# Batch 0's first keys through SyncE's queue in fp32, cast by VectorE, and another order of batch 0's last chunks

## The chip, the core and the metric

The kernel runs on one core of one Trainium2 chip. A core has a matmul engine (TensorE, "PE" in the profile; its weight loads are listed as "PEld"), VectorE ("DVE"), ScalarE ("ACT"), GpSimd ("POOL") and SyncE ("SP"). Sixteen DMA engines serve the core. GpSimd and SyncE each issue transfers into a queue of their own. The metric is the time on the device in microseconds (us): of the kernel before there are six runs, and their median is 365.86 us (365.17 to 366.24).

## The reference

Two blocks follow each other. The first is causal attention over 8 batches and 8 heads, with 576 queries and 64 values per head; 16 extra "beacon" keys and values, that every query may see, stand ahead of the 576 keys. The second is a feed-forward block on the 4608 tokens.

```python
k_all = np.concatenate([beacon_k, k], axis=2)
v_all = np.concatenate([beacon_v, v], axis=2)
scores = q @ k_all^T / sqrt(64)            # causal on the 576 keys
a = softmax(scores)
x = (a @ v_all), heads side by side        # 4608 x 512
out = (gelu(x @ w_gate) * (x @ w_val)) @ w_out     # 512 -> 1536 -> 512
```

All inputs and the output are fp32. The kernel computes in bf16 and accumulates in fp32.

## The kernel before, in words

The heads of a batch are taken two at a time: pair `m` is heads 2m and 2m+1, one on partitions 0 to 63 and one on 64 to 127. For a pair the kernel needs queries and keys with the head's 64 dimensions on partitions, so they are transposed. Batch 0 has nothing before it that could hide this, and so it is done by matmuls against an identity: `load_qk6` (its transfers go through `dma`, L111, on GpSimd's queue, and turn fp32 into bf16 on the way) brings two heads of q or k into `qk6` as 96 partitions of 6 rows; `tr_part` makes twelve transposes of it (L176) and one more for the beacon keys; `transpose_half` copies the outcome from PSUM into `qkT`, by VectorE (L213), or for pair 0's queries by ScalarE (through the helper at L171); `beacon_part` (L217) copies the 16 beacon columns. `transpose_both(b, m)` does keys first, then queries. Where ScalarE makes the copy, `transpose_half` puts eight transposes of a zero tile (`idle`) in front, whose outcome nobody reads.

A score tile is written by `scores`, called `c` for batch 0. A pair's causal triangle is cut into four chunks: `(m, 0)` to `(m, 2)` are 512, 496 and 464 columns for each of two heads, `(m, 3)` is 208 columns, and `(0, 3), (1, 3)` share one tile. TensorE computes the chunk and adds the mask by small matmuls with `eye` and `neg`; ScalarE then takes the exponential of the whole tile (L171). `av_head` multiplies the exponentials of one head with the values, `av` those of both heads of a pair; VectorE divides by the sum (L332, L334). `turn` transposes the normalised pair back, `put` copies it into `xT_sb`, from which the feed-forward matmuls (`gv_mms`) read.

PSUM sets what may run ahead: score tiles, the tiles of `av` and the tiles of `gv_mms` take turns in the pool `psum_s` with three buffers; a new one waits until the reader of the third before it is done. `psum_t` and `psum_o` have one buffer each, for transposes and for `av_head`.

The order on every engine is the order in which the program is written (`keep`). At the start it is this. SyncE issues the beacon keys and values of batch 0 in fp32 (L474, L476). GpSimd issues k of heads 0 and 1, q of heads 0 and 1, k of heads 2 and 3, then makes `eye` (the identity, L480), then goes on with q of heads 2 and 3, the other four loads of q and k, five loads of v, and the weights. VectorE clears tiles, casts the two beacon tiles (L517, L518) and makes `neg` from `eye` (L519, L520). TensorE runs 66 matmuls on the zero tile (`warm(66)`) and then pair 0's transposes. From there on chunks and transposes of the four pairs alternate, as written out by hand in the diff's last part. The rest of the program, 8 batches in which attention and feed-forward matmuls alternate, is not touched.

Of the kernel before, what the change touches and what calls it, by code (L numbers as in the profile page):

```python
# [7 lines left out]
P = 128  # L8
B, H, S, NB, D = 8, 8, 576, 16, 64
SK = S + NB  # L10
N_TOK = B * S
D_MODEL = 512
# [28 lines left out]
FP32 = mybir.dt.float32  # L41
# [8 lines left out]
def kernel(  # L50
# [12 lines left out]
    nc = tc.nc  # L63
    keep = tc.keep_in_program_order
# [8 lines left out]
    opool = ctx.enter_context(tc.tile_pool(name="opool", bufs=2))  # L73
    psum_s = ctx.enter_context(tc.tile_pool(name="psum_s", bufs=3, space=bass.MemoryType.PSUM))
    psum_t = ctx.enter_context(tc.tile_pool(name="psum_t", bufs=1, space=bass.MemoryType.PSUM))
# [16 lines left out]
    q_ring, k_ring, v_ring = [], [], []  # L92
# [17 lines left out]
    def dma(out_ap, in_ap):  # L110
        keep(nc.gpsimd.dma_start(out=out_ap, in_=in_ap))  # L111

    qk6 = {}

    def qk6_of(b):
        if b not in qk6:
            qk6[b] = (
                hpool.tile([P, 2, H, 6 * D], BF16, name="qk6", tag="hT_sb"),
                kpool.tile([NB, H, D], BF16, name="kb", tag="kb"),
            )  # L120
        return qk6[b]

    def load_qk6(b, h0, h1, ws=(1, 0)):
        for w in ws:
            src = (q, k)[w]
            dma(
                qk6_of(b)[0][0:96, w, h0:h1, :],
                src[b, h0:h1, :, :].rearrange("h (p r) d -> p h (r d)", r=6),
            )
# [37 lines left out]
    def mm(out_ap, lhsT, rhs, start, stop, **kw):  # L167
        keep(nc.tensor.matmul(out_ap, lhsT, rhs, start=start, stop=stop, **kw))  # L168

    def act(out_ap, in_ap, func, **kw):  # L170
        keep(nc.scalar.activation(out_ap, in_ap, func, **kw))  # L171


    def tr(out_ap, in_ap):
        n = in_ap.shape[0]
        keep(nc.tensor.transpose(out_ap, in_ap, ident[0:n, 0:n]))  # L176

    def tr_part(b, m, w, dst):
        qk, kb = qk6[b]
        for r in range(6):  # L180
            for hi in range(2):
                tr(
                    dst[64 * hi : 64 * hi + 64, r * 96 : (r + 1) * 96],
                    qk[0:96, w, 2 * m + hi, r * D : (r + 1) * D],
                )
        if w:
            tr(dst[:, S:SK], kb[:, 2 * m : 2 * m + 2, :])
# [14 lines left out]
    def transpose_half(b, m, w, by_act=False):  # L202
        pool, tag = ((psum_o, "o"), (psum_t, "t"))[w]
        t_ps = pool.tile([P, 1024], BF16, name="t_ps", tag=tag)
        for _ in range(8 if by_act else 0):
            tr(t_ps[0:D, 640:768], idle[:, 0:D])
        tr_part(b, m, w, t_ps)
        out_ap = qkT[:, m, w, NB:SK].rearrange("p (t r) -> p t r", r=6)
        in_ap = t_ps[:, 0:S].rearrange("p (r t) -> p t r", r=6)
        if by_act:  # L210
            act(out_ap, in_ap, ACT.Copy)
        else:
            keep(nc.vector.tensor_copy(out_ap, in_ap))  # L213
        return t_ps

    def beacon_part(m, t_ps):
        keep(nc.vector.tensor_copy(qkT[:, m, 1, 0:NB], t_ps[:, S:SK]))  # L217

    def transpose_both(b, m):
        k_ps = transpose_half(b, m, 1)  # L220
        transpose_half(b, m, 0, by_act=m == 0)
        beacon_part(m, k_ps)

    def warm(n):
        w_ps = psum_s.tile([P, 2, 512], FP32, name="w_ps", tag="s")
        for j in range(n):
            mm(w_ps[:, 0, 0:D], idle[:, 0:P], idle[:, 0:D], True, True)
# [10 lines left out]
    def scores(b, *parts):  # L238
        s_ps = psum_s.tile([P, 2, 512], FP32, name="s_ps", tag="s")
        c0 = 0  # L240
        for m, c in parts:
            score_mms(b, m, c, s_ps[:, :, c0 : c0 + CHUNK_W[c]])
            c0 += CHUNK_W[c]
        (m, c), n = parts[0], len(parts)
        o, w = CHUNK_OFF[c], CHUNK_W[c]
        act(
            exp_ring[:, m : m + n, :, o : o + w].rearrange("p g h c -> p h g c"),
            s_ps[:, :, 0 : n * w].rearrange("p h (g c) -> p h g c", g=n),
            ACT.Exp,
            scale=QK_SCALE,  # L250
        )
        if b:
            for m, c in parts:
                masks(b, m, c)
# [54 lines left out]
    def attend(b, m, hi, x_ps):  # L309
        expT, v_sb = exp_ring[:, m, :, :], v_ring[b % NRING]  # L310
        for j in range(5):
            for t in range(j + 1):
                e0 = EXP_OFF[t] + (j - t) * P
                mm(
                    x_ps[:, j * DV : (j + 1) * DV],
                    expT[0 : KROWS[t], hi, e0 : e0 + P],
                    v_sb[0 : KROWS[t], t, 2 * m + hi, 0:DV],
                    t == 0,
                    t == j,
                    skip_group_check=True,  # L320
                )
# [3 lines left out]
    def normalize(b, m, x_ps, h0, h1):  # L325
        i = b * NPAIR + m
        if h0 == 0:
            y_of[i] = ypool.tile([P, 5, 2, D], BF16, name="y_sb", tag="y_sb")
        r_sb = npool.tile([P, 2, 5, 1], FP32, name="r_sb", tag="r_sb")
        x = x_ps[:, :, 0 : 5 * DV].rearrange("p b (j d) -> p b j d", d=DV)  # L330
        r = r_sb[:, h0:h1, :, :]
        keep(nc.vector.reciprocal(r, x[:, :, :, D:DV]))  # L332
        keep(
            nc.vector.tensor_tensor(  # L334
                out=y_of[i][:, :, h0:h1, :].rearrange("p j b d -> p b j d"),
                in0=x[:, :, :, 0:D],
                in1=r.to_broadcast([P, h1 - h0, 5, D]),
                op=ALU.mult,
            )
        )  # L340

    def av(b, m):
        x = psum_s.tile([P, 2, 512], FP32, name="x_ps", tag="s")
        for hi in range(2):
            attend(b, m, hi, x[:, hi, :])
        normalize(b, m, x, 0, 2)

    def av_head(b, m, hi, pool, tag):
        x = pool.tile([P, 1, 512], FP32, name="x_ps", tag=tag)
        attend(b, m, hi, x[:, 0, :])  # L350
        normalize(b, m, x, hi, hi + 1)
# [108 lines left out]
    def out_mms(ci, u0, u1):  # L460
        for u in range(u0, u1):
# [8 lines left out]
                if ci >= N_CHUNKS - 2:  # L470
                    store(nc.sync)

    kb_sb = opool.tile([NB, H, D], FP32, name="kb_sb", tag="o_sb")
    keep(nc.sync.dma_start(out=kb_sb, in_=beacon_k[0].rearrange("h t d -> t h d")))  # L474
    vb_sb = opool.tile([NB, H, D], FP32, name="vb_sb", tag="o_sb")
    keep(nc.sync.dma_start(out=vb_sb, in_=beacon_v[0].rearrange("h t d -> t h d")))  # L476
    load_qk6(0, 0, 2)
    load_qk6(0, 2, 4, (1,))
    keep(
        nc.gpsimd.affine_select(  # L480
            out=eye,
            in_=eye,
# [4 lines left out]
            channel_multiplier=-1,  # L487
        )
    )
    load_qk6(0, 2, 4, (0,))  # L490
    load_qk6(0, 4, 6)
    load_qk6(0, 6, H)
    for load in key_loads(v, beacon_v, v_ring[0][:, :, :, 0:D], 0)[1:]:
# [18 lines left out]
    def c(*parts):  # L512
        scores(0, *parts)

    keep(nc.scalar.preload_act_table_set(SET_EXP))
    warm(66)
    keep(nc.vector.tensor_copy(qk6[0][1], kb_sb))  # L517
    keep(nc.vector.tensor_copy(v_ring[0][0:NB, 0, :, 0:D], vb_sb))  # L518
    keep(nc.vector.tensor_tensor_scan(neg, eye, idle, -1.0, ALU.add, ALU.add))  # L519
    keep(nc.vector.tensor_scalar_mul(neg, neg, -MASKED))  # L520
    transpose_both(0, 0)
    c((0, 0))
    c((0, 2))
    transpose_both(0, 1)
# [8 lines left out]
    c((2, 2))  # L533
    c((2, 1))
    c((3, 0))
    c((3, 2))
    av_head(0, 0, 0, psum_t, "t")
    av_head(0, 0, 1, psum_o, "o")
    c((2, 3), (3, 3))
    av(0, 1)  # L540
    c((3, 1))
    av(0, 2)
    turn(0, 0)
    put(0, 0, by_act=True)
# [123 lines left out]
```

The softmax here doesn't subtract the row's maximum and nothing guards it: scores larger than these inputs give would overflow.

## Time and profile before

| What | Value |
|---|---|
| median of six runs | 365.86 us |
| the profiled execution's own time | 365.73 us |
| its span, first to last instruction | 363.9 us |
| TensorE busy | 357.2 us, 98% of the span |
| ScalarE, GpSimd, VectorE busy | 52%, 44%, 43% |
| TensorE on the chain that ended last | 97% |
| TensorE busy from 0 to 21.84 us (before the first feed-forward matmul) | 18.4 of 21.84 us |
| TensorE busy from 21.84 us on | 338.9 of 342.2 us |

The span leaves out what lies before the first and after the last instruction, 1.8 us in this execution. A row of the timeline gives the start in us, the time taken (of all instructions merged into the row), the engine, the line, the operation and its tiles out<-in, and, in brackets, how long the engine sat idle before it and what ended that. Transfers are listed where they are issued; the time to landing runs from the start of the issue.

### The profile page before, as it was taken

How to read it: one execution, taken by the hardware profiler on the slowest of the kernel's cores; microseconds unless marked ns; L12 is line 12 of the kernel's file. 1: busy time of each engine (PE TensorE's matmuls, PEld its weight loads, DVE VectorE, ACT ScalarE, POOL GpSimd, SP SyncE). 2: the span in 40 equal slices, each digit the busy share in tenths (PEclk: the TensorE clock that was granted, in tenths of full speed). 3: DMA queues.
4: the chain of work that ended last, by engine and by line, in shares of the span. 5: the costliest groups of instructions: out<-in, count | busy, mean ns of one | idle time of the engine just before them, and what ended most of it. 6: DMA issues, size and time to landing. Idle time of an engine off the chain costs nothing.

```text
span 363.9 us, 7670 instructions
## 1 busy us (share of the span) xinstructions
PE 357.2 (98%) x3170; PEld 184.7 (51%) x3170; DVE 155.3 (43%) x305; ACT 189.0 (52%) x243; POOL 161.3 (44%) x288
## 2 busy tenths in 40 slices
PE   7899999999999999999999999999999999999996
PEld 7664446444654455444644464446544554444443
DVE  4546546343453335443534354334444353333332
ACT  3963488237923594349623891379335953321210
POOL 8934487555536552846374554556330530000000
PEclk9999999999999999999999999999999999999999
DMA  8999999899169954999299927993795032000103
GB/s 108 177 204 204 195 120 97 123 171 193 26 126 141 215 51 73 151 210 83 57 142 207 130 38 118 167 195 35 112 144 126 19 65 111 0 0 31 58 35 111
DMA packets 160419, 41.57 MB, mean 114 GB/s; under 512 B 146944, under 2 KB 155904, under 8 KB 160384
## 3 DMA queue, kind: packets, MB, share of 16 engines
q0 software_dynamic: 104848, 19.11, 68.6%
q1 hardware_dynamic: 55536, 21.96, 29.6%
q8 instruction: 25, 0.41, 0.5%
q14 instruction: 10, 0.08, 0.1%
HBM read 38.27 MB, written 9.44 MB: 131 GB/s over the span
## 4 chain that ended last, share of the span: by engine, by line
PE 97%; DVE 2%; issue 0%; ACT 0%; DVEq 0%
PE gv_ps L168 48%; PE o_ps L168 26%; PE x_ps L168 9%; PE s_ps L168 8%; PE t_ps L176 2%; PE v_ps L168 2%; PE g_ps L168 2%; DVE qkT L213 1%; PE w_ps L168 1%; PE y_ps L176 0%; DVE hT_sb L426 0%; ACT qkT L171 0%; DVE o_sb L445 0%; DVE qkT L217 0%; DVE idle L80 0%
## 5 line engine op out<-in xcount | busy, mean ns | idle before, releaser
L171 ACT ACTIVATE ge_sb<-gv_ps 128x512 bf16<-128x512 f32 x101 | 59.4, 597 | 142.8 <-PE gv_ps L168 141.7
L426 DVE TENSOR_TENSOR hT_sb<-gv_ps,ge_sb 128x512 bf16<-128x512 f32 x101 | 69.0, 691 | 113.5 <-ACT ge_sb L171 111.1
L168 PE MATMUL gv_ps<-xT_sb,wg_sb 128*128 128x512 bf16 x404 | 111.5, 379 | 0.0
L168 PE MATMUL gv_ps<-xT_sb,wv_sb 128*128 128x512 bf16 x404 | 111.5, 379 | 0.0
L168 PE MATMUL o_ps<-wo_sb,hT_sb 128*128 128x512 bf16 (+2 forms) x444 | 104.7, 373 | 0.0
L171 ACT ACTIVATE expT<-s_ps 128x992 bf16<-128x992 f32 (+3 forms) x112 | 100.6, 974 | 5.9 <-PE s_ps L168 4.7
L298 POOL TENSOR_SCALAR_AFFINE_SELECT expT<-expT 128x256 bf16<-128x256 bf16 (+1 forms) x140 | 52.3, 392 | 48.2 <-ACT expT L171 46.0
L168 PEld LDWEIGHTS <-wv_sb 128*128 128x128 bf16 x432 | 42.2, 98 | 50.6
L168 PEld LDWEIGHTS <-wg_sb 128*128 128x128 bf16 x432 | 42.0, 98 | 50.0
L168 PEld LDWEIGHTS <-hT_sb 128*128 128x128 bf16 x444 | 39.9, 98 | 41.7 <-issue 1.7
L168 PEld LDWEIGHTS <-expT 128*128 128x128 bf16 (+1 forms) x960 | 33.6, 97 | 9.8 <-DVE y_sb L334 2.9
L445 DVE COPY o_sb<-o_ps 128x512 f32<-128x512 f32 (+2 forms) x37 | 24.9, 672 | 31.2 <-PE o_ps L168 30.3
L168 PE MATMUL x_ps<-v_sb,expT 128*128 128x65 bf16 (+1 forms) x960 | 37.5, 193 | 0.0
L111 POOL DMA_DIRECT2D v_sb<-in_v_dram x40 | 33.6, 857 | 5.9 <-DMA wv_sb<-in_moe_w_val_dram 1.8
L168 PE MATMUL s_ps<-qkT 64*128 64x80 bf16 (+5 forms) x528 | 33.0, 250 | 2.4 <-DVE qkT L217 1.6
L111 POOL DMA_DIRECT2D k_sb<-in_k_dram x30 | 25.2, 843 | 16.6 <-DMA q_sb<-in_q_dram 11.6
L334 DVE TENSOR_TENSOR y_sb<-x_ps,r_sb 128x320 bf16<-128x320 f32 (+1 forms) x47 | 28.8, 612 | 1.6
L111 POOL DMA_DIRECT2D q_sb<-in_q_dram x30 | 25.3, 875 | 7.6 <-DMA v_sb<-in_v_dram 3.8
L332 DVE RECIPROCAL r_sb<-x_ps 128x5 f32<-128x5 f32 (+1 forms) x47 | 9.6, 204 | 42.1 <-PE x_ps L168 42.1
L168 PEld LDWEIGHTS <-qkT 64*128 64x128 bf16 x528 | 17.1, 95 | 18.1 <-issue 13.0
L377 POOL COPY hold_sb<-xT_sb 128x2 bf16<-128x2 bf16 x6 | 1.1, 186 | 31.2 <-DMA xT_sb<-y_sb 31.2
L610 ACT ACT_TABLE_LOAD x7 | 9.0, 1283 | 0.1
(54 smaller groups left out, 117.7 us busy)
## 6 DMA issues: line engine op xcount, KB each, us to landing
out_dram<-o_sb SPq DMA_DIRECT2D x35, 256.0 KB, 7.3
v_sb<-in_v_dram POOLq DMA_DIRECT2D x24, 128.0 KB, 9.5
q_sb<-in_q_dram POOLq DMA_DIRECT2D x18, 128.0 KB, 12.5
k_sb<-in_k_dram POOLq DMA_DIRECT2D x18, 128.0 KB, 5.8
wo_sb<-in_moe_w_out_dram POOLq DMA_DIRECT2D x3, 512.0 KB, 14.4
wg_sb<-in_moe_w_gate_dram POOLq DMA_DIRECT2D x2, 512.0 KB, 12.3
wv_sb<-in_moe_w_val_dram POOLq DMA_DIRECT2D x2, 512.0 KB, 13.9
v_sb<-in_v_dram POOLq DMA_DIRECT2D x8, 112.0 KB, 5.8
```

The costliest lines, as they stand in the source:

```text
L111: keep(nc.gpsimd.dma_start(out=out_ap, in_=in_ap))
L168: keep(nc.tensor.matmul(out_ap, lhsT, rhs, start=start, stop=stop, **kw))
L171: keep(nc.scalar.activation(out_ap, in_ap, func, **kw))
L176: keep(nc.tensor.transpose(out_ap, in_ap, ident[0:n, 0:n]))
L213: keep(nc.vector.tensor_copy(out_ap, in_ap))
L298: nc.gpsimd.affine_select(out=d, in_=d, pattern=[[0, 2], [1, n]], compare_op=ALU.is_ge, fill=0.0, base=0, channel_multiplier=-1,)
L332: keep(nc.vector.reciprocal(r, x[:, :, :, D:DV]))
L334: nc.vector.tensor_tensor(out=y_of[i][:, :, h0:h1, :].rearrange("p j b d -> p b j d"), in0=x[:, :, :, 0:D], in1=r.to_broadcast([P, h1 - h0 ...
L377: keep(nc.gpsimd.tensor_copy(hold_sb, x[:, 0 : S : S - 1]))
L426: nc.vector.tensor_tensor(out=h_of[ci][:, fi, :], in0=gv_of.pop((ci, fi))[1], in1=ge_sb, op=ALU.mult)
L445: keep(nc.vector.tensor_copy(o_sb[:, ti, c0:c1], o_ps))
L610: keep(nc.scalar.preload_act_table_set(SET_GELU))
```

## The change

1. One fp32 tile `raw` takes the place of the two small tiles for the beacons. SyncE's queue now starts with k of heads 0 and 1, as fp32, and then brings the two beacon tiles. VectorE casts those keys into `qk6` (the new L520 of the changed program). GpSimd's queue no longer has this load: it starts with q of heads 0 and 1, makes `eye`, and goes on with k and q of heads 2 and 3.
2. On VectorE `neg` is made first, then come the cast of the keys, the cast of the beacon keys, pair 0's transposes' copies, and after those the cast of the beacon values.
3. `warm` has 60 matmuls in place of 66, and four idle transposes stand ahead of pair 0's queries in place of eight.
4. Near the end of batch 0's attention the first `av_head` moves ahead of chunk `(3, 2)`, and chunk `(3, 1)` moves ahead of `av(0, 1)`.

```diff
@@ transpose_half
-        for _ in range(8 if by_act else 0):
+        for _ in range(4 if by_act else 0):
             tr(t_ps[0:D, 640:768], idle[:, 0:D])
@@ start
-    kb_sb = opool.tile([NB, H, D], FP32, name="kb_sb", tag="o_sb")
+    raw = opool.tile([P, 4, D_MODEL], FP32, name="raw", tag="o_sb")
+    k0_sb = raw[0:96, 0:2, 0 : 6 * D]
+    keep(nc.sync.dma_start(out=k0_sb, in_=k[0, 0:2, :, :].rearrange("h (p r) d -> p h (r d)", r=6)))
+    kb_sb, vb_sb = (raw[0:NB, g, :].rearrange("t (h d) -> t h d", h=H) for g in (2, 3))
     keep(nc.sync.dma_start(out=kb_sb, in_=beacon_k[0].rearrange("h t d -> t h d")))
-    vb_sb = opool.tile([NB, H, D], FP32, name="vb_sb", tag="o_sb")
     keep(nc.sync.dma_start(out=vb_sb, in_=beacon_v[0].rearrange("h t d -> t h d")))
-    load_qk6(0, 0, 2)
-    load_qk6(0, 2, 4, (1,))
+    load_qk6(0, 0, 2, (0,))
     keep(
         nc.gpsimd.affine_select(
...
     )
-    load_qk6(0, 2, 4, (0,))
+    load_qk6(0, 2, 4)
     load_qk6(0, 4, 6)
@@ compute
     keep(nc.scalar.preload_act_table_set(SET_EXP))
-    warm(66)
-    keep(nc.vector.tensor_copy(qk6[0][1], kb_sb))
-    keep(nc.vector.tensor_copy(v_ring[0][0:NB, 0, :, 0:D], vb_sb))
+    warm(60)
     keep(nc.vector.tensor_tensor_scan(neg, eye, idle, -1.0, ALU.add, ALU.add))
     keep(nc.vector.tensor_scalar_mul(neg, neg, -MASKED))
+    keep(nc.vector.tensor_copy(qk6[0][0][0:96, 1, 0:2, :], k0_sb))
+    keep(nc.vector.tensor_copy(qk6[0][1], kb_sb))
     transpose_both(0, 0)
+    keep(nc.vector.tensor_copy(v_ring[0][0:NB, 0, :, 0:D], vb_sb))
     c((0, 0))
@@ last chunks
     c((3, 0))
+    av_head(0, 0, 0, psum_t, "t")
     c((3, 2))
-    av_head(0, 0, 0, psum_t, "t")
     av_head(0, 0, 1, psum_o, "o")
     c((2, 3), (3, 3))
+    c((3, 1))
     av(0, 1)
-    c((3, 1))
     av(0, 2)
     turn(0, 0)
```

## The prediction

> **What bounds the kernel now.** I read the chain of waits first, since it says where a microsecond counts. From 15.4 us to the end it stays on TensorE almost without a break; what the change can win must come from the stretch before. So I asked for the chain of the first 30 us.
>
> ```profile
> 1.13 3.70 PE w_ps L168 x66
> 4.83 1.67 PE t_ps L176 x24
> ...
> 6.52 0.66 ACT qkT L171
> ...
> 7.22 0.76 PE s_ps L168 x12
> ...
> 15.44 0.90 PE s_ps L168 x12
> 16.34 1.02 PE x_ps L168 x30
> ...
> 18.83 0.71 PE s_ps L168 x13
> 19.54 1.02 PE x_ps L168 x30
> ```
>
> The first 7.2 us are one line: warm-up, pair 0's transposes, ScalarE's copy, first chunk. To see what lets the transposes start I took the timeline of the first 7 us, of GpSimd, VectorE and TensorE in turn.
>
> ```profile
> 1.38 0.77 POOL L111 DMA_DIRECT2D qk<-in_k_dram  x1 [0.86 <-POOLq L652]
> 2.14 0.64 POOL L111 DMA_DIRECT2D qk<-in_q_dram  x1
> 2.76 0.64 POOL L111 DMA_DIRECT2D qk<-in_k_dram  x1
> 3.48 0.54 POOL L480 TENSOR_SCALAR_AFFINE_SELECT eye<-eye 128x256 bf16<-128x256 bf16 x1
> 3.97 0.66 POOL L111 DMA_DIRECT2D qk<-in_q_dram  x1
> ```
>
> ```profile
> 4.05 0.69 DVE L519 TENSOR_TENSOR_SCAN neg<-eye,idle 128x256 bf16<-128x256 bf16 x1 [0.29 <-POOL eye L480]
> 4.78 0.23 DVE L520 TENSOR_SCALAR neg<-neg 128x256 bf16<-128x256 bf16 x1
> ```
>
> ```profile
> 4.79 0.69 PE L176 MATMUL t_ps<-eye,qk 96*64 96x96 bf16 x12
> ...
> 5.53 0.58 PE L176 MATMUL t_ps<-eye,idle 128*64 128x128 bf16 x6
> ...
> 6.02 0.46 PE L176 MATMUL t_ps<-eye,qk 96*64 96x96 bf16 x10
> ```
>
> The keys are issued at 1.38 and land 3.4 us later by the transfer list, at 4.78; the transposes start at 4.79. The last warm-up matmul starts at 4.59 and they are 0.053 apart, so the array is free at 4.65: the keys' landing, not the warm-up, starts the transposes. Then comes ScalarE:
>
> ```profile
> 7.74 11.50 ACT L171 ACTIVATE expT<-s_ps 128x1024 bf16<-128x1024 f32 x13 [0.56 <-PE s_ps L168]
> 19.58 1.00 ACT L171 ACTIVATE expT<-s_ps 128x992 bf16<-128x992 f32 x1 [0.34 <-PE s_ps L168]
> ```
>
> Thirteen exponentials run back to back. TensorE, VectorE's copies and ScalarE form one pipeline from 7.7 to 20 us, in which an earlier start moves everything.
>
> **What the Trainium skill says.** "DMA: Bandwidth & Descriptors", section "SWDGE vs HWDGE vs iDMA": only GpSimd's queue can cast in flight, and SyncE's needs no software to write descriptors. That fits: the 32 KB beacon tile on SyncE's queue lands 1.8 us after its issue, GpSimd's first load 3.4 us. "SBUF — State Buffer", section "Who interferes with whom": a VectorE cast that uses both ports locks GpSimd out, so that it can't write descriptors. The trace does not show it: the beacon cast of 2.68 to 3.14 lies over the issue at 2.76, which takes 0.64 us like the others. "TensorE: Matmul & The Clock Gate", "Part 1": the array runs at half clock until one free-running window of about 3.4 us has been busy. It agrees: pair 0's key transposes start 0.080 apart, two at a time, later ones 0.042, and the trace's clock record has full clock from 5.68 us.
>
> **Step 1, the keys' path.** SyncE issues them at 0.82, where the first beacon tile is issued now. That one carried 32 KB in 1.8 us. The keys are 288 KB in fp32. The loads of q and k land 1.02 us apart on average while they stream (4.78 to 11.89 us for eight), so I add about 1 us: landing at 3.6. Lower end 3.0 (the queue was almost idle until 2.75); upper end 4.2 (3.4 us after the issue, as GpSimd's). The cast then needs VectorE. GpSimd's first issue now ends at 2.15, `eye` takes from the end of an issue (3.40) to 4.02 now, 0.62, so it is ready at 2.77; the scan starts 0.03 later, and from there to the end of the scaling it is 0.96 (4.05 to 5.01): VectorE is free at 3.76. Landing at 3.6 is hidden behind that. The cast: no row has it. The beacon casts of 512 elements took 0.46 and 0.41. "VectorE: DVE Perf Modes", "The perf-mode tier table", puts an fp32 copy at two elements per cycle, and "Side-by-side" has about 150 cycles fixed at 0.96 GHz: 512 gives 0.42, which agrees, and 768 gives 0.56. At one element per cycle it would be 0.96. I take 0.56: done at 4.32. Sixty warm-ups end at 1.13 + 60 x 0.0533 = 4.33. Both meet; with the 0.04 that now lie between landing and start, the transposes start at 4.37, **0.42 earlier** (bounds: 0.46, when only the warm-up counts, and 0). The beacon cast follows, to 4.78; its transpose stands 0.62 behind the first, at 4.99.
>
> **Step 2, the idle transposes.** From the first key transpose to the first idle one it is 0.74 (4.79 to 5.53), so now they begin at 5.11. Eight took about 0.54: two at half clock (0.107 apart), six at 0.056. Four at half clock take 0.43. The clock does not come earlier because the program does, so pair 0's queries, which ran at full clock, would now begin at 5.54, with two of their six steps at 0.08: last start 5.82, ready 6.03 against 6.48. **Steps 1 and 2 together: 0.45**; the copy on ScalarE starts that much sooner. Were the clock to come after 7 us in both, the eight would cost 0.86, the four 0.43, and the gain is 0.85. Since the window runs freely, executions will differ; I take 0.50, near the lower end, because any clock before about 6.3 gives 0.45 to 0.6. The queries have landed: they are issued first on GpSimd's queue, at 1.38, so at about 4.8.
>
> **Step 3, what moves with GpSimd's queue.** Keys of heads 2 and 3 are issued at 2.77 as now; q of these heads at 3.41 instead of 3.97, and all later ones about 0.6 earlier, since one issue of 0.64 left the queue. Pair 1's queries land at 8.27 now and are used at 8.40; now they are wanted at 7.90 and would land at 7.7 (the same 4.3 us after the issue). Pairs 2 and 3 have 0.8 us and more to spare. The last v load, issued at 10.54, lands at 15.87; now about 0.65 sooner, 15.2. The first `av_head` needs that only in its last step, at about 15.8. The cast of the beacon values moves behind L217, where VectorE idled 2.04 us: nothing, while it is under that. SyncE's queue has nothing else until the first store.
>
> **Step 4, the last chunks.** In the old times, from `c((3, 0))` at 15.44 to the first `turn` at 20.40, TensorE is on the chain. Now: first `av_head` 15.89, `(3, 2)` 16.45, second 16.84, shared chunk 17.41, `(3, 1)` 17.87 to 18.25. It takes 0.38 there, like `(0, 1)` at 8.78, and not the 0.71 it has on the chain now. But `av(0, 1)` now takes the buffer of `(3, 2)`, whose exponential ends at 18.48: 0.27 of wait. It runs to 19.45, `av(0, 2)` to 20.38, so `turn(0, 0)` is where it was; `turn(0, 1)` needs VectorE's 0.22 and 0.82 on pair 1, now over at 20.72, and waits 0.1. ScalarE's gap of 0.34 closes, but nobody waits for it. Sum: **0.10 later**. Bounds: 0.3 sooner (the whole saving, if ScalarE's buffer comes free in time) to 0.25 later.
>
> **Sum.** -0.50 + 0.10 = -0.40 us. From 21.84 us on TensorE is busy 338.9 of 342.2 us, so the gain is kept. The profiled execution's own time is 365.73 (span 363.9): 365.33. The median of the runs is 0.13 above it: 365.86 - 0.40 = **365.46**, I say 365.45.
>
> **The rivals.** (a) *Casts starve GpSimd; slower.* The two casts cover 3.76 to 4.78, just where q of pair 1 and k of pair 2 are issued. If they hold up descriptors for their whole 1.0 us, pair 1's queries land at 8.7; wanted at 7.90, they cost 0.8, and with step 4: -0.50 + 0.80 + 0.10 = +0.40, 366.25. It decides from 0.2 us of hold-up on and is a loss from 0.6. Against: the issue at 2.76 under a cast. For: that cast had 16 partitions, and the landing of pair 1's queries comes 1.7 us after the load before, the longest step among the eight. (b) *The keys are no earlier.* Landing at 4.2, or a cast of 0.96: transposes start at 4.75 to 4.8, the idle transposes alone gain 0.1, step 4 takes it: 365.85. For: [...]GpSimd's first load took 3.4 us. (c) *More than I count.* A late full clock (0.85) and step 4 at -0.1: 364.9. For: six runs that spread over 1.07 us although nothing in the program varies.
>
> **Chances.** Forecast 0.50 (365.1 to 365.7), (c) 0.23, (b) 0.16, (a) 0.11. Under 0.2% (0.73 us) a measurement of this kernel tells little from no change; faster by more means under 365.13: (c) and the forecast's edge, 0.28. Slower by more means over 366.59: the upper part of (a), 0.05. Same: 0.67. For 8 in 10 the range takes in (b) and the middle of (a) and (c): 364.8 to 366.2.
>
> **What would show it.** In the profile after: the key cast of about 0.56 us ending near 4.3; the first key transpose near 4.37 and ScalarE's first copy near 6.05; GpSimd's issue of pair 1's queries near 3.4 with a duration of 0.64; thirteen exponentials starting near 7.25 and no gap before the fourteenth; a wait of TensorE on ScalarE before `av(0, 1)`; the first feed-forward matmul near 21.4. An issue on GpSimd stretched to over 1 us beside a cast proves (a); a key transpose after 4.7 proves (b). A first feed-forward matmul that is 0.4 earlier with no shorter total would mean that something later takes it back, which I hold to be unlikely.

## The result: 368.74 us, slower, and the profile after

The changed kernel's median is **368.74 us** (18 runs, 366.3 to 369.78); the kernel before, run beside it, stayed at 365.86 (37 runs, 365.17 to 367.02). By the medians the change costs 2.9 us where I forecast a gain of 0.4. (The ratio, 1.0061 with a 95% interval of 1.0048 to 1.0074, is that of the means, 368.11 and 365.89; here and below it differs from the medians' where the runs form groups.) They do so here: by their spans, 7 of the 18 runs have 364.1 to 364.8 us and 11 have 366.1 to 367.3. The times of the first group are 366.3 to 367.72 (median 366.6), of the second 368.13 to 369.78 (368.87). The profiled execution, 369.3 us with a span of 367.3, is of the second.

First the chain of waits of the first 30 us, as the prediction showed it of the kernel before.

```profile
1.38 4.97 DMA qk<-in_q_dram
...
6.39 0.71 PE t_ps L176 x12
...
7.12 0.66 ACT qkT L171
...
7.83 1.32 PE s_ps L168 x12
```

Warm-up and key transposes have left the chain; what starts pair 0 is now the transfer of its *queries*, 4.97 us. One chunk takes 1.32 us where it took 0.76. The timeline of the start shows how it came to that (start, time taken, engine, line, operation, tiles, and in brackets the idle time and what ended it).

```profile
0.82 0.40 SPq L475 DMA_DIRECT2D raw<-in_k_dram  x1
...
1.13 3.38 PE L168 MATMUL w_ps<-idle 128*128 128x64 bf16 x60 [1.13 <-DVE idle L80]
...
4.18 0.70 DVE L520 CAST qk<-raw 96x768 bf16<-96x768 f32 x1 [0.54 <-DMA raw<-in_k_dram]
...
4.93 0.50 PEld L176 LDWEIGHTS <-qk 96*64 96x64 bf16 x12 [0.58 <-DVE qk L520]
4.93 0.69 PE L176 MATMUL t_ps<-eye,qk 96*64 96x96 bf16 x12 [0.42 <-DVE qk L520]
...
6.39 0.51 PEld L176 LDWEIGHTS <-qk 96*64 96x64 bf16 x12 [0.32 <-DMA qk<-in_q_dram]
...
7.83 0.61 PE L168 MATMUL s_ps<-qkT 64*128 64x512 bf16 x2 [0.74 <-ACT qkT L171]
```

The brackets are what to read. VectorE, done with `neg`, waits 0.54 us for the keys, which land at 4.16 by the transfer list; TensorE, done with 60 warm-ups, then stands still before the keys, 0.4 us by its matmuls and 0.6 by its weight loads, and 0.3 us before the queries. In the kernel before, the weight loads of the warm-up ran until 0.12 us before those of the key transposes. And everything TensorE does afterwards is slow: a chunk's first two matmuls take 0.61 us, where the kernel before has this row.

```profile
7.22 0.39 PE L168 MATMUL s_ps<-qkT 64*128 64x512 bf16 x2 [0.75 <-ACT qkT L171]
```

Two rows of the changed kernel say until when.

```profile
16.14 0.69 PE L176 MATMUL t_ps<-eye,qk 96*64 96x96 bf16 x12
...
16.88 0.45 PE L176 MATMUL t_ps<-eye,qk 96*64 96x96 bf16 x12
```

The same twelve transposes take 0.69 us at 16.14 and 0.45 at 16.88. The trace's clock record has the full clock from 16.80 us here, and from 5.68 in the kernel before. What lies between shows in the busy times of 5.6 to 16.8 us (columns: stretch, length, then busy us and count of PE, PEld, DVE, ACT and POOL, the clock, and two of DMA), before and after:

```profile
5.60:16.80 11.20, 8.86 (x214) 6.61 (x215) 5.32 (x11) 9.62 (x12) 11.14 (x16) 1.00 1.65 165
```

```profile
5.60:16.80 11.20, 10.22 (x152) 7.09 (x150) 4.14 (x9) 7.13 (x9) 10.52 (x15) 1.00 1.68 172
```

TensorE is *more* busy, 10.22 us for 8.86, and does 152 matmuls instead of 214. (The 1.00 behind the engines is the mean clock as the view works it out; it reads 1.00 also where the record has no entry yet, so the durations are what to read.) ScalarE, the other end of the pipeline, breaks up: thirteen exponentials back to back before, now groups of two and of three, each with 0.86 us of waiting ahead of it, and nine back to back only from 14.97 us, after 0.83 us of waiting.

```profile
8.63 1.86 ACT L171 ACTIVATE expT<-s_ps 128x1024 bf16<-128x1024 f32 x2 [0.86 <-PE s_ps L168]
11.35 2.79 ACT L171 ACTIVATE expT<-s_ps 128x992 bf16<-128x992 f32 x3 [0.86 <-PE s_ps L168]
```

The first feed-forward matmul starts at 24.82 us instead of 21.84. From there to the end it is 342.5 us against 342.07. That second, small difference is in the costliest groups, whose last column had been 0.0 for this one:

```profile
L168 PE MATMUL gv_ps<-xT_sb,wg_sb 128*128 128x512 bf16 x404 | 111.5, 379 | 0.6 <-DMA xT_sb<-y_sb 0.6
```

It is one wait, at 71 us, for a transposing transfer (from batch 1 on `turn` transposes by DMA, L367), which the timeline shows:

```profile
71.31 0.38 PE L168 MATMUL gv_ps<-xT_sb,wg_sb 128*128 128x512 bf16 x1 [0.59 <-DMA xT_sb<-y_sb]
```

So two places cost time: the clock at the start, and a transfer at 67 us that the change does not touch. The experiments take them apart.

### The profile page after: what moved, and what is told of

It reads as the page before. It is cut to its first block, busy times and chain, and to the rows that moved or that the text cites. A ratio compares the mean times of both kernels' runs of the same rounds, so it can differ in the third digit from the quotient of the medians.

```text
span 367.3 us, 7651 instructions
## 1 busy us (share of the span) xinstructions
PE 360.6 (98%) x3160; PEld 186.6 (51%) x3160; DVE 155.9 (42%) x306; ACT 189.1 (51%) x243; POOL 160.8 (44%) x287
## 4 chain that ended last, share of the span: by engine, by line
PE 94%; DMA 2%; ACT 1%; DVE 1%; issue 0%; POOLq 0%
PE gv_ps L168 47%; PE o_ps L168 25%; PE x_ps L168 8%; PE s_ps L168 8%; PE t_ps L176 2%; PE v_ps L168 2%; PE g_ps L168 2%; DMA qk<-in_q_dram 1%; DMA xT_sb<-y_sb 1%; ACT expT L171 1%; DVE qkT L213 0%; PE y_ps L176 0%; DVE y_sb L334 0%; ACT qkT L171 0%; DVE o_sb L445 0%
## 5 line engine op out<-in xcount | busy, mean ns | idle before, releaser
L168 PE MATMUL s_ps<-qkT 64*128 64x80 bf16 (+5 forms) x528 | 34.5, 258 | 1.4 <-ACT qkT L171 0.7
L168 PEld LDWEIGHTS <-qkT 64*128 64x128 bf16 x528 | 17.4, 96 | 16.8 <-issue 12.7
```

## Experiments

"Matmul count" is the number of warm-up matmuls and idle transposes together, 74 before (66 + 8) and 64 after (60 + 4). "Wait" is a wait of TensorE on `xT_sb<-y_sb` after 30 us, "clock" the first entry of full clock in the profiled execution.

### The whole change with the holes filled

```diff
-    warm(60)
+    warm(72)
-        for _ in range(4 if by_act else 0):
+        for _ in range(8 if by_act else 0):
```

> The changed kernel with 72 warm-up matmuls and 8 idle transposes in place of 60 and 4, so that TensorE has no hole of 0.6 us before the key transposes and of 0.3 us before the query transposes. Theory A (the holes keep the array at half clock, until 16.8 us in the profile of after): full clock comes before 8 us, and the time falls by about 2 us to 366.3 to 366.6, what is left being the later landing of the queries. Theory B (the new order of the last chunks costs the time): stays at 368 to 369. Theory C (the later landings alone cost it): stays near 368.5.

Measured: 365.63 us (13 runs, 365.18 to 366.14) beside 365.82; ratio 0.9992 [0.998, 1.0004]. Nothing else differs from the changed kernel, and all of the 2.9 us is gone. (The count is now 80, too, so that the transfer at 67 us may be mended along with the clock; runs further down take the two apart.) The time is below the 366.3 to 366.6 expected, so the later queries do not cost what was reckoned for them. Its timeline:

```profile
4.95 0.45 PE L176 MATMUL t_ps<-eye,qk 96*64 96x96 bf16 x12
...
7.07 0.39 PE L168 MATMUL s_ps<-qkT 64*128 64x512 bf16 x2 [0.75 <-ACT qkT L171]
```

The keys are no earlier (4.95), but no idle time stands in brackets before them, the transposes take 0.45, the clock comes at 4.72, and no wait is left later.

### The new order of the last chunks alone

```diff
     c((3, 0))
+    av_head(0, 0, 0, psum_t, "t")
     c((3, 2))
-    av_head(0, 0, 0, psum_t, "t")
     av_head(0, 0, 1, psum_o, "o")
     c((2, 3), (3, 3))
+    c((3, 1))
     av(0, 1)
-    c((3, 1))
```

> The kernel before with nothing but the new order of the last chunks of batch 0. Theory A and theory C: 365.7 to 366.1, within 0.2 us of before. Theory B: 367.5 or more.

Measured, on the kernel before: 366.08 us (21 runs, 365.38 to 366.82) beside 365.82; ratio 1.0009 [1.0002, 1.0015]. It costs 0.26 us. The wait is where the prediction put it, before `av(0, 1)`, of 0.28 us:

```profile
18.25 2.01 PE L168 MATMUL x_ps<-v_sb,expT 128*128 128x65 bf16 x60 [0.28 <-ACT expT L171]
```

### The shorter cover alone

```diff
-    warm(66)
+    warm(60)
-        for _ in range(8 if by_act else 0):
+        for _ in range(4 if by_act else 0):
```

> The kernel before with nothing but 60 warm-up matmuls and 4 idle transposes; the keys still come through GpSimd's queue. TensorE then has a hole of 0.45 us before the key transposes. Theory A: in part of the executions full clock comes late, and the times spread over 2 us or more, median 366 to 368. Theories B and C: 365.6 to 365.9, little else than the shorter idle part.

Measured, on the kernel before, loads and order untouched: 368.93 us (10 runs, 366.03 to 370.86) beside 365.82; ratio 1.0073 [1.0044, 1.0102]. The fewer idle matmuls alone reproduce the whole loss, more than the 366 to 368 expected, in two groups again, with the clock at 17.05 and a wait of 0.67 us at 70.4:

```profile
4.72 0.69 PE L176 MATMUL t_ps<-eye,qk 96*64 96x96 bf16 x12 [0.20 <-DMA qk<-in_k_dram]
...
7.32 0.61 PE L168 MATMUL s_ps<-qkT 64*128 64x512 bf16 x2 [0.75 <-ACT qkT L171]
```

### The load through SyncE alone, cover as before

```diff
# against the changed kernel: order of the last chunks as before, and
-    warm(60)
+    warm(66)
-        for _ in range(4 if by_act else 0):
+        for _ in range(8 if by_act else 0):
```

> The changed kernel with the old order of the last chunks, 66 warm-up matmuls and 8 idle transposes: the load through SyncE and the cast alone. The hole before the key transposes is 0.28 us. Theory A: full clock before 8 us, time 366.2 to 366.7 by the queries' landing at 6.35. Theory C: 368 to 369, as after. Theory B: 366.2 to 366.7 too; e1 and e2 tell B from A.

Measured: 365.51 us (14 runs, 365.19 to 367.15) beside 365.82; ratio 0.9995 [0.9986, 1.0005]. The load does no harm (366.2 to 366.7 was expected), and its key transposes start at 4.93. The profiled execution happened to be the slowest, 367.15: its clock record has full clock at 4.15, half from 7.56, full again from 14.39. So full clock can also come early and be lost. The loss shows between two rows, a chunk's first two matmuls of 0.42 us and its next two of 0.63:

```profile
7.32 0.42 PE L168 MATMUL s_ps<-qkT 64*128 64x512 bf16 x2 [0.74 <-ACT qkT L171]
...
7.65 0.63 PE L168 MATMUL s_ps<-qkT 64*128 64x464 bf16 x2
```

The three times lie one and two steps of 3.41 us apart. Half clock for two such steps makes the mean granted clock of this run 0.991. In the changed kernel 4 of the 11 late runs have such a mean (0.990 or 0.991) and 7 have 1.00, as its profiled execution has, whose record has no entry before 16.80. So both kinds seem to occur there. Now and then the kernel before has such a run too: one of the 45 beside the next version took 368.59 us, at a mean of 0.985.

### Filled, with the old order

```diff
# the load alone, and
-    warm(66)
+    warm(72)
```

> The changed kernel with 72 warm-up matmuls, 8 idle transposes and the old order of the last chunks. Theory A (the clock; the new order costs the 0.26 us of e2): 365.63 - 0.26, so 365.2 to 365.5. If the new order costs nothing once the start is filled: 365.6, as e1.

Measured: 365.43 us (14 runs, 365.13 to 365.97) beside 365.91; ratio 0.999 [0.9982, 0.9998]. No late group, no wait.

### Beacon values off SyncE's queue

```diff
# filled, old order, and
-    keep(nc.sync.dma_start(out=vb_sb, in_=beacon_v[0].rearrange("h t d -> t h d")))
-    for load in key_loads(v, beacon_v, v_ring[0][:, :, :, 0:D], 0)[1:]:
+    for load in key_loads(v, beacon_v, v_ring[0][:, :, :, 0:D], 0):
-    keep(nc.vector.tensor_copy(v_ring[0][0:NB, 0, :, 0:D], vb_sb))
```

> e5 with the beacon values brought by GpSimd's queue ahead of the other values, cast on the way; SyncE's queue keeps the keys and the beacon keys. If the beacon tiles' small packets share the DMA engines with the queries and hold them back, the queries of pair 0 land 0.3 us or more before the 5.54 to 6.35 of the profiles with the fp32 load, and the time is 365.0 to 365.3; if it is the fp32 keys that hold them back, the landing stays and the time is that of e5.

Measured: 365.78 us (14 runs, 365.17 to 366.29) beside 365.91; ratio 0.9997 [0.9989, 1.0004]. The queries land at 5.07 us in its profile, as against 5.49 in that of the version it was made from, and 5.49 to 6.35 in all nine profiles with the beacon values on SyncE's queue. But a later version with the same loads as this one (the last of the experiments) has them at 5.68. So it is not shown that the beacon values hold them up. The time did not follow either: a miss, taken up below.

### Half of the cover given back, two ways

```diff
# against the changed kernel, first
-    warm(60)
+    warm(72)
# or second
-        for _ in range(4 if by_act else 0):
+        for _ in range(8 if by_act else 0):
```

> The changed kernel with 72 warm-up matmuls and still 4 idle transposes: the hole before the key transposes is gone, the one before the query transposes stays. Theory A, each hole a part of it: between the two, median 365.8 to 367.5 with some executions above 367.5. If the first hole alone decides: 365.6, as e1.

> The changed kernel with 60 warm-up matmuls and 8 idle transposes: the hole of 0.6 us before the key transposes stays, the one before the query transposes is gone. Theory A, each hole a part of it: 366 to 368 with some executions above 367.5. If the first hole alone decides: 368.5, as after; if the second alone: 365.6.

Measured: warm-up alone (count 76) 367.16 us (8 runs, 366.52 to 369.62), ratio 1.0049 [1.0028, 1.007]; idle transposes alone (count 68) 366.27 (22 runs, 365.41 to 369.5), ratio 1.0023 [1.0006, 1.004], both beside 365.91. In the second, 4 of 22 runs lie above 368: a shorter hole, fewer late clocks. The first surprised me: its start is good (first feed-forward matmul at 21.94), and it loses 1.31 us in one wait at 184.5 us:

```profile
185.79 0.38 PE L168 MATMUL gv_ps<-xT_sb,wg_sb 128*128 128x512 bf16 x1 [1.31 <-DMA xT_sb<-y_sb]
```

So the wait on a transposing transfer seems to be a cause of its own that moves with the number of matmuls, which the next runs put to the test.

### Three runs on the count alone

```diff
# first: the changed kernel with count 80, in another split
-    warm(60)
+    warm(76)
# second: the kernel before with two matmuls more, count 76
-    warm(66)
+    warm(68)
# third: the kernel before with ten matmuls fewer, as long in time: count 64
-            mm(w_ps[:, 0, 0:D], idle[:, 0:P], idle[:, 0:D], True, True)
+            w = 2 * D if j < 10 else D
+            mm(w_ps[:, 0, 0:w], idle[:, 0:P], idle[:, 0:w], True, True)
-    warm(66)
+    warm(56)
```

> The changed kernel with 76 warm-up matmuls and 4 idle transposes: as many TensorE instructions as e1 (80 of these matmuls). Theory D (the place of an instruction fetch against the fourth transposing DMA of a batch, which the number of TensorE instructions sets, costs e7 its 1.3 us at 184 us): that wait is gone, lowest times 365.2 to 365.5, median 365.5 to 366.2, the rest being executions with late full clock. If e7 is slow through its hole before the query transposes alone: 367 as e7.

> The kernel before with 68 warm-up matmuls in place of 66, so with as many TensorE instructions as e7; no hole. Theory D: a wait of TensorE for the transposing DMA of about 1.3 us near 184 us, every execution 1 us or more above before: 366.9 to 367.3. Theory A (the clock alone): 365.9, as before.

> The kernel before with 10 warm-up matmuls of 128 columns and 46 of 64 in place of 66 of 64: the same length of warm-up with 10 matmuls fewer, so as many TensorE instructions as after and e3. Theory D: the wait of 0.6 us near 68 us that after and e3 show, 366.4 to 366.6, hardly spread. Theory A: 365.9.

Measured, beside 365.86: 365.46 us for count 80 (19 runs, 364.98 to 366.31; ratio 0.999 [0.9983, 0.9996]); 366.84 for two matmuls more (12 runs, 366.28 to 368.5; 1.0028 [1.0018, 1.0039]); 366.85 for ten fewer (12 runs, 366.43 to 370.05; 1.0032 [1.0017, 1.0048]). **Two matmuls of 53 ns at the start cost 1 us**, and not there: the wait is at 184.5 us in the kernel with two more and at 68.0 in the one with ten fewer. (The first wait is half as long as expected; the kernel with ten fewer is 0.2 us above what was expected, and more spread.)

```profile
185.06 0.38 PE L168 MATMUL gv_ps<-xT_sb,wg_sb 128*128 128x512 bf16 x1 [0.61 <-DMA xT_sb<-y_sb]
```

```profile
68.48 0.38 PE L168 MATMUL gv_ps<-xT_sb,wg_sb 128*128 128x512 bf16 x1 [0.51 <-DMA xT_sb<-y_sb]
```

The DMA view from the issue of that transposing DMA (180.9 us) until TensorE goes on, first in the kernel with two matmuls more (a queue with its packets, MB and share of the engines' time; an issue with its time to landing), then from the same issue in the filled version, where the view has no line of q8 (its one packet of instructions, 8 KB on q14, starts as the transfer ends):

```profile
q8 instruction: 1, 0.02, 1.6%
...
xT_sb<-y_sb SPq DMA_TRANSPOSE x1, 4.1
```

```profile
xT_sb<-y_sb SPq DMA_TRANSPOSE x1, 2.6
```

A single packet of 16 KB on the instruction queue q8 starts 1.7 to 2.0 us after the transposing DMA was issued, and the DMA takes 4.1 us instead of 2.6. In all 18 profiles, the fourth transposing DMA of a batch, the one that TensorE then waits for, has such a packet beside it five times, lands after 4.1 to 4.8 us each time, and those are the five profiles with the wait; of the others, all land within 2.9 us but one, which took 3.2. The changed kernel has its packet at 67.1 us:

```profile
q8 instruction: 1, 0.02, 1.3%
...
xT_sb<-y_sb SPq DMA_TRANSPOSE x1, 4.2
```

The program's own instructions are fetched by DMA, and the number of TensorE's instructions ahead decides beside which transfer a fetch falls: the wait is near 70 us in the three profiles with count 64, near 184 in the two with 76, and nowhere in the others. The same coincidence holds beyond the fourth. A batch has four transposing DMAs, a profile 28, and of the 504 in all 18 profiles 99 have a packet on q8 that starts 0.4 to 2.2 us after their issue: every one of them takes 2.9 to 5.5 us. Of the 382 with no packet on q8 between issue and landing, 374 take 2.5 to 2.8 us and the others 2.8 to 3.6. That the fetch *causes* the delay is still inferred from this; moving a fetch with the count unchanged was not tried.

### Each cause without the other

```diff
# first: the kernel before with warm(60), and six matmuls put back at 35 to 43 us, count 74
+        for _ in range(2 if by_act else 0):
+            tr(t_ps[0:D, 0, 640:656], idle[0:NB, 0:D])
-    warm(66)
+    warm(60)
# second: the changed kernel, holes and all, with ten put back there, count 74
+        for _ in range((4, 3, 3)[m] if by_act else 0):
+            tr(t_ps[0:D, 0, 640:656], idle[0:NB, 0:D])
```

> The kernel before with 60 warm-up matmuls and six idle transposes of 16 columns added between 35 and 43 us, so that only the hole before the key transposes is new and the number of TensorE instructions by 43 us is that of before. Theory A: a part of the executions has late full clock, median 366.1 to 367, highest above 368; lowest times near 365.3. Theory D alone: 366.0, no more spread than before.

> The changed kernel with ten idle transposes of 16 columns added between 35 and 43 us and nothing else: its two holes stay, the number of TensorE instructions from 43 us on is that of before. Two causes: the wait near 70 us goes, the lowest times fall from 366.3 to 365.6 to 365.9 (0.3 us for the ten transposes), while a part of the executions stays 2 us and more above them by late full clock; median 366 to 368.5. If the clock were all of it: lowest times 366.3 or more. If the fetch were all of it: 365.8 with no spread.

Measured: the hole at the old count 366.31 us (22 runs, 365.59 to 368.96; ratio 1.0027 [1.0011, 1.0042]), of which 16 lie at 365.59 to 366.63 and 6 at 368.75 to 368.96. The changed kernel at the old count 367.68 (22 runs, 365.71 to 369.1; 1.0039 [1.0024, 1.0055]): 8 at 365.71 to 366.02 and 14 at 367.23 to 369.1. Neither profile has the wait. So the count moves the lower group, from 366.6 to 365.84 in the changed kernel, and leaves the two groups standing; the holes make the groups. (Of the 14, 8 have a mean clock of 0.991 to 0.995, so by the reckoning above an early full clock that was lost, and lie at 367.23 to 367.82; the other 6 lie above 368.) The profiled execution of the second was one of the lower group, and its hole was short, with the clock at 6.01:

```profile
4.68 0.69 PE L176 MATMUL t_ps<-eye,qk 96*64 96x96 bf16 x12 [0.17 <-DVE qk L522]
```

### The best split with the old order

```diff
# the changed kernel, with the order of the last chunks as before, and
-    warm(60)
+    warm(76)
```

> The changed kernel with 76 warm-up matmuls, 4 idle transposes and the old order of the last chunks (e9 with the old order). If the new order costs its 0.26 us of e2 here too: 365.2 to 365.3. If it costs nothing here: 365.4 to 365.5, as e9. In both cases no wait of TensorE for a transposing DMA and full clock before 8 us.

Measured: 365.57 us (22 runs, 365.12 to 367.13) beside 365.97; ratio 0.9992 [0.9983, 1.0]. With the start mended, the new order is 0.2 us worse in one pair (365.63 to 365.43) and 0.1 better in the other (365.46 to 365.57, which stood beside 365.86 and 365.97): not resolved there.

### Where the mended versions win

They are 0.2 to 0.5 us ahead of the kernel before (ratios 0.999 to 0.9992; two of the four intervals reach 1.0) with keys no earlier. Their profiles have it after the first feed-forward matmul: 341.74 to 341.77 us to the end against 342.07. The chain of waits of the kernel before has this at 46 us:

```profile
46.06 0.02 DVEq L426
46.08 0.46 issue
46.54 0.70 DVE hT_sb L426
```

VectorE's semaphore is met at 46.06, and its multiplication starts at 46.54, with nothing that it waits for in between. The versions with the key cast and the beacon-value cast, one VectorE instruction more than before, don't have it; the miss above had dropped a cast, and has it again, with 342.03 us to the end. So I added one short instruction to the kernel before and to that miss:

```diff
-    nc.vector.memset(qkT[:, :, 0, 0:NB], 0.0)
+    for _ in range(2): nc.vector.memset(qkT[:, :, 0, 0:NB], 0.0)
```

> The kernel before, with one VectorE instruction more: the clearing of the 16 beacon columns stands there twice (0.1 us or less, at the start, while VectorE has nothing due). Nothing else differs. Theory A (what the mended versions won, 0.35 to 0.4 us, comes from the number of VectorE's instructions: with one more, the place in the program at which VectorE has to wait for its own next instructions moves, and the 0.48 us that it starts late on L426 near 46.5 us, with TensorE behind it, are gone): about 365.5, and L426 starts there within 0.1 us of its v_ps. Theory B (the win comes from the load through SyncE's queue or from the order at the start): as before, 365.8 to 366.0, and the late start stays.

> The version in which the beacon values come by GpSimd's queue (365.78 measured, where 365.43 was measured for the same program with that load on SyncE's queue and one VectorE cast more), with the clearing of the beacon columns written twice, so that VectorE has as many instructions as in the version at 365.43. Theory A (the missing instruction moved VectorE's late start back to L426 near 46.5 us): 365.4 to 365.5, late start gone. Theory B (the load's place cost it): 365.8 again, late start still there or not.

Measured, beside 365.99: 366.05 us (13 runs, 365.19 to 366.75; ratio 0.9995 [0.9983, 1.0007]) and 365.74 (22 runs, 364.95 to 366.1; 0.9989 [0.9983, 0.9995]). The late start is gone in both. The chain of the kernel before with one more:

```profile
46.85 0.69 PE o_ps L168 x3
47.55 0.73 PE s_ps L168 x10
```

The chain no longer leaves TensorE, and the stretch after the first feed-forward matmul is 341.79 and 341.81 us. So the instruction count does decide that delay: of the 18 profiles, the 7 with as many VectorE instructions as before have it, the 11 with one more don't. In single executions it is worth some 0.3 us: without the wait on a transposing DMA and without matmuls put in later, the stretch is 342.01 to 342.07 us to the end in the profiles that have it, 341.74 to 341.81 in those that don't. That it decides the median *time* is not shown: the second run fell below the kernel before as expected (in absolute terms it missed the 365.4 to 365.5), the first did not, its median is where it was, and its interval holds both a gain of 0.6 us and a loss of 0.3. Whether the 0.35 us of the mended versions is this delay, the start, or some of both stays open.

## Why the prediction was wrong

**Step 2 is the step that failed.** It said "The clock does not come earlier because the program does", and asked only what a given clock does to the idle transposes. It allowed for a late clock only in both kernels alike, as a larger gain. That the clock could come *later* because the change opens holes was never asked. I had quoted the Trainium skill for just this ("TensorE: Matmul & The Clock Gate", "Part 1": a free-running window of some 3.4 us must have been busy), and not applied it. The traces agree on the step: 4.15, 7.56 and 14.39 in one record are one and two times 3.41 us apart. From the changed kernel's 16.80 I reckon back in such steps: its windows ended at 13.39, 9.97 and 6.56. The one from 3.14 to 6.56 holds both holes, 0.9 us by the weight loads, and failed; the kernel before's, from 2.27 to 5.68, holds one of 0.12, and passed. The next holds the 0.74 us in which TensorE waits for ScalarE's copy, which every version has. I read from this that there is one good window ahead of the copy, and when it fails, full clock comes three windows, ten us, later. The price is the distance between the groups: 368.87 - 366.6 = 2.3 us, in 11 of 18 executions.

What a window must hold to pass is not shown, and it is not idle time alone. The window from 0.38 to 3.79 of the kernel with two matmuls more passed, though the warm-up began only at 1.13; the one from 3.39 to 6.81 of the shorter cover failed with a hole of 0.36 us by the weight loads. The changed kernel's window from 9.97 to 13.39 failed with a single wait of 0.16 us in its matmuls. The first of these holds nothing but warm-up matmuls, the second is two thirds transposes, the third transposes and score matmuls; whether the kind of work counts was not tried. That filling the holes cures it is measured; how large a hole may be is not.

**Step 1** failed in all three terms, and that made the first hole. Landing: 3.6 expected, 4.16 measured, 3.34 us after the issue (2.9 to 3.6 in the eleven profiles with this load); no better than the keys' 3.1 to 3.4 through GpSimd's queue, and near the upper bound of 4.2. Cast: 0.56 expected, 0.70 measured (and 0.56 in the filled version: the estimate from the Trainium skill's "VectorE: DVE Perf Modes", "The perf-mode tier table", was met there and not here). Key transposes: 4.37 expected, 4.93 measured, and 4.68 to 5.30 in every version with this load. I took the cover of 60 matmuls as just long enough, "Both meet"; the bound that I kept for the landing would have opened the hole, and I priced it at no gain instead of asking what idles meanwhile.

**Also in Step 2**, "The queries have landed" at 4.8: they landed at 6.35. GpSimd's issue was as early as I said, 1.38, but its transfer took 5.0 us where the first one had taken 3.4. The transfer list shows it slowed: between 4.25 and 5.0 us the 768-byte packets of GpSimd's queue numbered 18 to 32 per quarter of a us (54 to 67 in the kernel before), while the beacon tiles' packets of 256 bytes came through SyncE's queue, behind the keys, until 5.8; in the kernel before these were done by 2.8. But the two versions without the beacon values on that queue had the queries at 5.07 and 5.68, so the cause stays open.

**Step 3** held for the issues and not for the landings. Pair 1's queries were issued at 3.24 instead of 3.97 and landed at 8.50, not at 7.7 (8.24 before); the last v load landed at 15.78, not at 15.2 (15.87 before). As for rival (a), GpSimd's issues beside the key cast take 0.63 us here like the others, so this profile by itself does not show the lock that the Trainium skill describes ("SBUF — State Buffer", "Who interferes with whom"). Other profiles suggest that one of the two waits for the other. In that of the version with the idle transposes alone given back, the issue during which the cast starts is stretched:

```profile
3.85 0.92 POOL L111 DMA_DIRECT2D qk<-in_k_dram  x1
4.08 0.56 DVE L520 CAST qk<-raw 96x768 bf16<-96x768 f32 x1 [0.45 <-DMA raw<-in_k_dram]
```

In three profiles that issue takes 0.88 to 0.92 us and ends 0.13 or 0.14 after the cast, which takes 0.56. In five, this one among them, it takes 0.63, and the cast, which started at 4.11 to 4.25, ends at 4.87 or 4.88 each time and so takes up to 0.76. This fits the page's exclusive lock and would account for the 0.70 in Step 1; no run isolates it. It costs 0.2 to 0.3 us, and the hold-up of 1.0 that rival (a) reckoned with did not come. The kernel went slower by a mechanism that I did not list. Rival (b) was right on its facts (landing near 4.2, keys no earlier) and wrong on the time, since it too took the cover for free.

**Step 4**: mechanism right, with a wait of 0.28 for the expected 0.27; its size +0.26 for +0.10, at the upper bound of 0.25.

**The missing term** is the number of instructions. The change takes ten matmuls from TensorE's stream, and a fetch of instructions falls beside a transposing DMA at 67 us: about 1 us, as ten fewer (366.85) and two more (366.84) show on the kernel before. Together: about 1.0 in every execution and 2.3 in 11 of 18 gives a median 3.3 above the mended versions' 365.4 to 365.6, which is 368.7 to 368.9; 368.74 was measured.

## What to carry to other kernels

Idle matmuls that bridge a load are part of the clock's budget: shorten them only by what is *measured* to arrive earlier, and leave a margin for the late arrival, because the hole before the keys, 0.4 us by the weight loads in the kernel before with the old count, cost 2.8 us in 6 of 22 executions, and twelve to sixteen warm-up matmuls more, 0.6 to 0.9 us of them, left the best times. When two groups of run times appear, look for a threshold that single executions pass or miss, and compare the groups before explaining the median. And before a difference of 1 us is laid to an edit, look in the trace for one new wait far from it: a changed number of instructions alone can do that.

## What I had not expected of the hardware

- A fetch of 16 KB of instructions beside a transposing DMA goes with 2.9 to 5.5 us of it instead of 2.6 (all 99 cases in 18 profiles), and beside the fourth of a batch with 4.1 to 4.8 us and a wait of TensorE of 0.5 to 1.3 us; two matmuls more brought one beside such a fourth at 181 us.
- Full clock once reached was lost again: at 4.15, half from 7.56, full from 14.39; the window from 4.15 to 7.56 holds idle times of 0.35 us before the key transposes and 0.74 for ScalarE's copy.
- VectorE started one instruction some 0.5 us after its semaphore was met, at the same place of the program, near 46.5 us (48.9 where full clock came late), in all seven profiles with as many VectorE instructions as the kernel before; one more ahead of it removed it, one fewer brought it back.
- A 288 KB load on SyncE's nearly empty queue landed 3.34 us after its issue, no sooner than a load of the same tile by GpSimd's queue (3.4).
- A cast of fp32 by VectorE and an issue by GpSimd that overlap lengthened one or the other: the issue from 0.63 to 0.9 us, or the cast from 0.56 to as much as 0.76.
